# FFN1 units of four pairs and one block in 512-column steps, and a fixed order of TensorE's passes in the first third, in a fused attention and FFN kernel

## The chip, the cores and the metric

The kernel runs on one core of a Trainium2 chip. The metric is the device time of one execution in microseconds. Three runs of the kernel before took 151.54, 151.74 and 151.81 us, median 151.74. The core has a matrix engine (TensorE, PE in the profile; its weight loads are listed apart as PEld), a vector engine (DVE), a scalar engine (ACT), GpSimd (POOL), and queues that start DMAs (SP above all). Each engine works through its own list of instructions in order and waits for the others by semaphores.

## The reference

One layer norm feeds two branches, and the output is their sum with the input. S = 2048 tokens, D = 448, 16 heads of 28, F = 1792.

```
xn  = layernorm(x)                                   # no weights
q, k, v = split(xn @ wqkv)                           # per head
phi(t)  = concat(softmax(t @ w_phi), softmax(-(t @ w_phi)))
kv = phi(k)^T v ;  z = sum over tokens of phi(k)
A  = ((phi(q) kv) / (phi(q) z + 1e-6)) @ wo
B  = silu(xn @ w1) @ w2                              # FFN1, FFN2
out = x + A + B
```

All inputs and the output are bfloat16; products accumulate in float32.

## The kernel before

**Tiles.** The 2048 tokens are 16 tiles of 128, taken as 8 pairs (0 to 7). D is 3 blocks of 128 and one of 64. The normalised rows of a pair lie in `xn_sb` and are transposed on TensorE into `xnT`: `ln_pair` computes statistics (`bnst`, `bnag`, `ve` on DVE, `rstd` on GpSimd), normalises in three DVE instructions (`xn`), transposes in seven steps (`xnT_tr`) into a pair of PSUM banks, and copies these out (`xnT_ev`). PSUM has eight banks of 512 float32 columns; the code uses them in pairs.

**Steps and passes.** TensorE is used as two halves of 64 rows. A step is two matmuls that run side by side, one on each half (`mms`, line 445). `contract` (line 476) makes one product out of two passes: the first has 4 steps for each block of output, the second 3, and the second adds to what the first wrote with the halves exchanged, so all its steps wait on a semaphore until the last matmul of the first has ended (`o.syncs.add(prev.id)`). Between the two passes other work is wanted.

**FFN1.** `ffn1_chunk(p0, npair, f0, fend, units)` (line 745) makes units: one unit fills one pair of banks (2 x 512 columns) and ends in one SiLU of 1024 columns on ACT, which writes `hT`. With two pairs of tokens (`npair = 2`) a step has 256 columns and a unit holds two blocks of F; there are 14 blocks. `units` names the banks, in turn. Pairs 0 and 1 use `ffn1_single`; pairs 2 to 7 are 7 units for each two pairs, all with `npair = 2`: 13 of these 21 units come before the attention part, 8 behind its projections.

**Fold.** The weights of q and k are multiplied by w_phi on the chip: `fold_tr` transposes them in three sets of 24 matmuls (`wT_tr`), DVE copies each in two instructions (`wT_ev`) into `scr`, and `fold(kt)` multiplies (`fold_mm`, nine steps for each of four `kt`) into banks 6 and 7. Three DVE copies and one ACT copy (`fold_ev`) bring the result to `wqk_sb`.

**Attention part.** For each pair `k_macro` projects k and v (`pk_mm`, `v_mm`), `q_group` the queries (`pq_mm`, 512 columns); ACT takes exponentials (`exp_act`), DVE the sums, GpSimd the divisions, and `k_acc` adds to kv. ACT has one function table at a time: it loads the one for exponentials once, behind the last SiLU of the first part (`pre_exp`). Then the remaining FFN1 units run among the products of q and kv (`U_mm`), whose results DVE divides (`q_divide`), and last come FFN2 and the output projection pair by pair.

**Order.** A list scheduler (`schedule`, line 218) with estimated costs orders each engine's instructions; smaller numbers of an operation go first when several are ready. `odeps` fix an order within one engine without a semaphore. Before the change such fixed orders hold for the first pairs (`order0`), for the attention part (`chain`) and for the last unit with the transposes of pair 7 (`turn`, lines 920 to 923); between these (lines 879 to 919) the scheduler chooses. `ln_pair(6)` and `ln_pair(7)` stand at lines 909 and 916, behind the folds; they write banks 2 and 3, and 6 and 7. DMAs are issued in order on SP's queue, and `paced` (lines 1260 and 1261) holds some of the loads back until given copies are done.

Of the kernel before, what the change touches and what calls it, by code (L numbers as in the profile page):

```python
# [332 lines left out]
def bass_parallel_sum__linear_kernel_hedgehog__dense_activation_silu__prompt_kernel(  # L333
# [10 lines left out]
    S, D, H, DH, FF = 2048, 448, 16, 28, 1792  # L344
    NT, NPAIR = S // 128, S // 256
    KF = 3
    FT = FF // 128
# [8 lines left out]
    with es:  # L356
# [4 lines left out]
        NXN = 4  # L361
# [60 lines left out]
        P = _Prog()  # L422
# [105 lines left out]
        def warm(n, cols=256):  # L528

            one = [nc.const_aps.tensor(1.0, [64, 128], dtype=BF16, start_partition=64 * h) for h in range(2)]  # L530
            rhs = [a[:, None, :].broadcast_to([64, cols // 128, 128]) for a in one]
            dst = [banks[4 + h][:, 0:cols].rearrange("p (a c) -> p a c", c=128) for h in range(2)]
            k = len(P.ops)
            for i in range(n):
                mms([(dst[h], one[h], rhs[h], True, True) for h in range(2)], "warm", cols * 0.836)
            return P.ops[k:]
# [96 lines left out]
                    xn, x_sb[:, t, c0:c1], mv[:, t, 0:1], rstd[:, t:t + 1], ALU.subtract, ALU.mult),  # L633
                    reads=[x_sb[:, t, c0:c1], mv[:, t, 0:1], rstd[:, t:t + 1]], writes=[xn], name="xn")

        def ln_tr(p, js, b0, eng):
            for i, j in enumerate(js):
                trs([(bank16[b0 + h][:, 64 * i:64 * i + 64], xn_sb[r, p % NXN, 128 * j:128 * j + 128], r)
                     for h, r in enumerate((UP, LO))], "xnT_tr")
            n = len(js)  # L640
            src = psum16[:, b0 * 1024:(b0 + 2) * 1024].rearrange("p (b c) -> p b c", b=2)[:, :, 0:64 * n].rearrange(
                "p b (j u) -> p b j u", u=64)
            dst = xnT[:, js[0]:js[-1] + 1, p, :].rearrange("p j (b u) -> p b j u", b=2)
            if eng == "act":
                act(dst, src, ACTF.Identity, "xnT_ev")
            else:
                copy_dve(dst, src, "xnT_ev", d_dve(128 * n, 2))
# [8 lines left out]
                    reads=[xs, mv[:, tt, 0:1], rstd[:, tt:tt + 1]], writes=[dst], name="xn")  # L656

        def lnz_bank(p, t, j):
            return 6 if p else (2 * (j // 2) if t == 0 else 6 - 2 * (j // 2))

        def lnz_tr(p, t):
            k = len(P.ops)
# [61 lines left out]
                c.odeps.add(a.id)  # L724
            return ev

        def ln_pair(p, one_by_one=False):
            t0, t1 = 2 * p, 2 * p + 1
            for t in (t0, t1):
                ln_stats(t)  # L730
                if one_by_one:
                    ln_rstd(t, t + 1)
            if not one_by_one:
                ln_rstd(t0, t1 + 1)
            ln_norm(p, t0)
            ln_norm(p, t1)
            ln_tr(p, [0, 1, 2, 3, 4, 5, 6], {2: 2, 3: 4, NPAIR - 2: 2}.get(p, 6), "act" if p in LN_ACT else "dve")

        LN_ACT = (2,)
        silus = []  # L740
# [98 lines left out]
            copy_dve(wqk_sb[:, kt, 0, 0:7, 56:64], bA[:, 168:224].rearrange("p (g u) -> p g u", u=8), "fold_ev", d_dve(56))  # L839

        ev0, order0 = lnz_first()
        banks_ = iter((0, 2, 4, 0, 2, 4, 0, 6))
        evp, passes, ln_late = [], [], []
        for p in range(2):
            for f0, f1, i0, i1 in ((0, 6, 0, 2), (0, 6, 2, 3), (6, 10, 0, 2), (10, FT, 0, 2)):
# [30 lines left out]
        for a, c in zip(order0, order0[1:]):  # L876
            for o in c:
                o.odeps.add(a[-1].id)
        k = len(P.ops)
        ln_pair(4)  # L880
        later4 = [o for o in P.ops[k:] if o.eng == "dve"]
        tr4 = [o for o in P.ops[k:] if o.name == "xnT_tr"]
        evp.append(P.ops[-1])
        unit_no[0] = 0
        ffn1_chunk(2, 2, 0, 4, (4, 0, 2))
        k = len(P.ops)
        ln_pair(5)
        later5 = [o for o in P.ops[k:] if o.eng == "dve"]
        for o in later4 + later5:
            o.odeps.add(early_dve)  # L890
        for i in range(3):
            ffn1_chunk(2, 2, 4 + 2 * i, 6 + 2 * i, (4, 0, 2))
            fold_tr(3 * i)
        for o in tr4:
            o.odeps.add(units_done[2][0][-1].id)
        ffn1_chunk(2, 2, 10, FT, (4, 0, 2))
        P.cur_prio = 2
        late_constants()
        lnz_rest()
        P.cur_prio = 0  # L900
        for kt in range(4):
            ffn1_chunk(4, 2, 2 * kt, 2 + 2 * kt)
            k = len(P.ops)
            fold(kt)
            for o in P.ops[k:]:
                if o.eng == "pe":
                    o.odeps.add(units_done[-1][1][-1].id)
        k = len(P.ops)
        ln_pair(6)
        for o in P.ops[k:]:  # L910
            if o.eng == "dve":
                o.odeps.add([a for a in later4 if a.name == "xn"][-1].id)
        unit_no[0] = 0
        ffn1_chunk(4, 2, 8, 12, (0, 4))
        k = len(P.ops)
        ln_pair(7)
        for o in P.ops[k:]:
            if o.eng == "dve":
                o.odeps.add([a for a in later5 if a.name == "xn"][-1].id)
        turn = [units_done[-1][0], [o for o in P.ops if o.name == "xnT_tr"][-7:], units_done[-1][1]]  # L920
        for x, y in zip(turn, turn[1:]):
            for o in y:
                o.odeps.add(x[-1].id)

        def proj(p, W, b0, name):
            return contract([(lambda r, b: xnT[r, b, p, :], W,
# [1 line left out]

        def k_macro(p):
            sl = p % NEK  # L930
            kbk = {1: 4, 2: 6, 7: 6}.get(p, 0)
            k12 = proj(p, lambda r, k: wqk_sb[r, k, 1, :, 0:56], kbk, "pk_mm")
            kb = psum[:, kbk * 512:kbk * 512 + 1024].rearrange("p (t c) -> p t c", t=2)[:, :, 0:D]
            for s in range(2):
                exp_act(Ek[sl][:, :, s * D:(s + 1) * D], kb, 1.0 if s == 0 else -1.0, "exp_k")
            v12 = proj(p, lambda r, k: wv_sb[r, k, :], 2, "v_mm")
            vb = psum[:, 1024:2048].rearrange("p (t c) -> p t c", t=2)[:, :, 0:D].rearrange("p t (h d) -> p t h d", h=H)
# [88 lines left out]
        for p in range(NPAIR):  # L1026
# [12 lines left out]
            if p == 6:  # L1039
                chain += [k12[0], v12[0], k12[1], v12[1], k_acc(3)]  # L1040
            elif p == NPAIR - 1:
                chain += [k12[0], k_acc(4), v12[0], k12[1], v12[1], q12[0], k_acc(5), q12[1]]
            elif p > 2:
                chain += [k12[0], v12[0], k12[1], v12[1], q12[0], k_acc(p - 3), q12[1]]
            else:
# [149 lines left out]
        def marked(fn, *a):  # L1195
            k = len(P.ops)
            fn(*a)
            return [o for o in P.ops[k:] if o.eng == "pe"]

        out_order = []  # L1200

        def out_pair(p):
# [173 lines left out]
```

## Time and profile before

| what | value |
|---|---|
| runs | 151.54 to 151.81 us, median 151.74 |
| profiled execution | 151.56 us, of which the span is 149.81 us |
| first matmul of the attention part | 40.53 us from the span's start |
| FFN1, 256 columns | 744 matmuls from `xnT` and `w1_sb`, 46.0 us busy |
| weight loads of FFN1 | 768, 94 ns each |
| SiLU of a whole unit | 1.02 us each, 27 of them |

The span runs from the first to the last instruction of the core. Rows of the timeline have a start, a length, an engine, a line, the operation with output and input, their shapes, and a count of merged instructions; in brackets stands idle time ahead of the row, with what ended it. Matmuls overlap (the next starts before the last has left the array), so TensorE's pace is read from one row's start to the next row's, and a length of 0.27 us for a 256-column matmul isn't what it costs. Line 448 is the helper that issues all matmuls, so groups are told apart by tile names: `w_sb` in the profile stands for `w1_sb` and `w2_sb`, `EqT` also holds data of the first two pairs, `scr` the transposed weights.

### The profile page before, as it was taken

To read this page: it belongs to the slowest core of one execution; us is meant where nothing else is said; L and a number is where in the kernel's file an instruction comes from. 1 tells how busy PE (TensorE), PEld (TensorE's weight loads), DVE (VectorE), ACT (ScalarE), POOL (GpSimd) and SP (SyncE) were. 2 spreads that over 40 slices of the span, in tenths; PEclk is the share of its full clock that TensorE was granted. 3 is DMA by queue.
4 is the path that set the end of the run, shared out by engine and by line. 5 is a ranking of instruction groups with operands and counts; after the bars stand their busy time and mean duration, and the time that the engine had idled before them with its cause. 6 is when DMAs were issued, how large, how long until landed. Compare 5 with 4: busy or idle time off the path is not lost.

```text
span 149.8 us, 5945 instructions
## 1 busy us (share of the span) xinstructions
PE 145.9 (97%) x2698; PEld 97.1 (65%) x2698; DVE 100.1 (67%) x192; ACT 72.6 (48%) x83; POOL 56.2 (38%) x86
## 2 busy tenths in 40 slices
PE   7899999999999999999999999999999999999992
PEld 6798888888844444444488985555555555555672
DVE  1998888865518899777992677839393939392203
ACT  3657755568699887779488554202020202022000
POOL 7134131020102778876981064270707061614000
PEclk9999999999999999999999999999999999999999
DMA  4999374000004432353201000010101010101012
GB/s 120 354 263 256 100 218 131 4 4 4 4 0 123 127 123 68 87 132 45 33 4 21 4 4 0 4 61 4 61 4 61 7 61 4 61 0 66 0 66 61
DMA packets 9427, 10.30 MB, mean 69 GB/s; under 512 B 1626, under 2 KB 9018, under 8 KB 9402
## 3 DMA queue, kind: packets, MB, share of 16 engines
q1 hardware_dynamic: 9098, 9.71, 22.6%
q8 instruction: 21, 0.34, 0.9%
q10 hardware_dynamic: 304, 0.21, 0.5%
q14 instruction: 4, 0.03, 0.1%
HBM read 7.37 MB, written 1.84 MB: 61 GB/s over the span
## 4 chain that ended last, share of the span: by engine, by line
PE 94%; DVE 2%; DMA 1%; issue 0%
PE psum L448 91%; PE psum L461 3%; DMA x_sb<-in_A_x_dram 1%; DVE st L610 1%; DVE EqT L654 1%; DVE out_raw L1190 0%; DVE mv L614 0%; PE psum L1075 0%; DVE rstd L692 0%
## 5 line engine op out<-in xcount | busy, mean ns | idle before, releaser
L448 PE MATMUL psum<-xnT,w_sb 64*128 64x256 bf16 (+1 forms) x768 | 46.7, 268 | 0.0
L448 PE MATMUL psum<-w_sb,hT 64*128 64x448 bf16 (+2 forms) x504 | 46.5, 328 | 0.0
L448 PEld LDWEIGHTS psum<-xnT,w_sb 64*128 64x128 bf16 x768 | 35.5, 94 | 4.4
L467 ACT ACTIVATE hT<-psum 128x1024 bf16<-128x1024 f32 (+1 forms) x29 | 28.3, 993 | 14.4 <-PE psum L448 14.3
L1161 POOL TENSOR_TENSOR xn_sb<-wraw 128x448 bf16<-128x448 f32 (+4 forms) x39 | 20.6, 562 | 36.3 <-DVE wraw L1139 23.6
L448 PEld LDWEIGHTS psum<-w_sb,hT 64*128 64x128 bf16 x504 | 22.5, 94 | 16.6
L467 ACT ACTIVATE oT<-psum 128x896 bf16<-128x896 bf16 x8 | 7.3, 917 | 40.2 <-PE psum L461 40.2
L952 POOL TENSOR_TENSOR scr<-scr,Rk 128x1792 bf16<-128x1792 bf16 (+2 forms) x8 | 19.2, 2407 | 14.0 <-ACT scr L467 11.1
L1139 DVE TENSOR_TENSOR wraw<-psum,Gq 128x1792 f32<-128x1792 f32 (+1 forms) x10 | 16.4, 1650 | 0.9
L467 ACT ACTIVATE EqT<-psum 128x1024 bf16<-128x1024 f32 x14 | 13.6, 1021 | 3.9 <-PE psum L448 3.9
L1190 DVE TENSOR_TENSOR out_raw<-psum,x_sb 128x896 bf16<-128x896 f32 (+2 forms) x9 | 8.8, 980 | 9.5 <-PE psum L448 9.4
L1124 DVE RECIPROCAL R<-psum 128x64 f32<-128x64 f32 (+1 forms) x9 | 4.6, 511 | 15.2 <-PE psum L448 15.2
L448 PE MATMUL psum<-wv_sb,xnT 64*128 64x448 bf16 x112 | 13.7, 349 | 0.0
L448 PE MATMUL psum<-wo_sb,oT 64*128 64x448 bf16 (+2 forms) x126 | 13.6, 328 | 0.0
L448 PE MATMUL psum<-wqk_sb,xnT 64*128 64x448 bf16 x112 | 13.2, 349 | 0.0
L448 PE MATMUL psum<-xnT,wqk_sb 64*128 64x512 bf16 (+1 forms) x112 | 13.0, 378 | 0.0
L625 POOL TENSOR_TENSOR rstd<-ve,neghalf 128x2 f32<-128x2 f32 (+1 forms) x9 | 5.9, 651 | 17.4 <-DVE ve L624 17.4
L944 DVE TENSOR_REDUCE Sk<-scr 128x64 f32<-128x1792 bf16 (+1 forms) x8 | 12.3, 1532 | 0.2
L610 DVE BATCH_NORM_STATS2 st<-x_sb 128x6 f32<-128x448 bf16 x16 | 9.8, 615 | 3.2 <-DMA x_sb<-in_A_x_dram 3.2
L467 ACT ACTIVATE scr<-psum 128x896 bf16<-128x896 f32 x12 | 10.3, 913 | 2.4 <-PE psum L448 1.8
L471 DVE CAST scr<-psum 128x896 bf16<-128x896 f32 x6 | 6.5, 1080 | 6.2 <-PE psum L448 6.2
L448 PEld LDWEIGHTS psum<-wo_sb,oT 64*128 64x128 bf16 x126 | 5.9, 94 | 4.8 <-ACT oT L467 0.2
(78 smaller groups left out, 133.7 us busy)
## 6 DMA issues: line engine op xcount, KB each, us to landing
out_dram<-out_raw SPq DMA_DIRECT2D x7, 224.0 KB, 1.9
w_sb<-in_B_w_dram SPq DMA_DIRECT2D x3, 448.0 KB, 3.4
x_sb<-in_A_x_dram SPq DMA_DIRECT2D x2, 448.0 KB, 5.3
w_sb<-in_B_w_dram SPq DMA_DIRECT2D x2, 384.0 KB, 5.7
x_sb<-in_A_x_dram SPq DMA_DIRECT2D x3, 224.0 KB, 5.1
w_sb<-in_B_w_dram SPq DMA_DIRECT2D x3, 224.0 KB, 3.9
wraw<-in_A_wqkv_dram SPq DMA_DIRECT2D x1, 672.0 KB, 4.4
w_sb<-in_B_w_dram SPq DMA_DIRECT2D x1, 576.0 KB, 4.2
```

Of the source, the lines that this page charges most:

```text
L448: r = e.matmul(dst, lhsT, rhs, start=start, stop=stop, skip_group_check=True)
L461: out = e.transpose(dst, src, ident[r, 64:128] if r == LO else ident[r, 0:64])
L467: return P.op("act", d_act(_cols(src)), lambda e: e.activation(dst, src, func, scale=scale), reads=[src], writes=[dst], table=table, name= ...
L471: return P.op("dve", dur, lambda e: e.tensor_copy(dst, src), reads=[src], writes=[dst], name=name)
L610: P.op("dve", 600, lambda e: e.bn_stats(st6[:, t, :], x_sb[:, t, :]), reads=[x_sb[:, t, :]], writes=[st6[:, t, :]], name="bnst")
L625: P.op("pool", 580, lambda e: e.tensor_tensor(r2, v2, nh, ALU.pow), reads=[v2, nh], writes=[r2], name="rstd")
L944: P.op("dve", d_dve(896 * n), lambda e, S4=S4, E4=E4: e.tensor_reduce(S4, E4, AXL.X, ALU.add), reads=[E4], writes=[S3], name="Sk")
L952: lambda e, E5=E5, R5=R5: e.tensor_tensor(E5, E5, R5, ALU.mult),
L1124: P.op("dve", d_rec(32 * n), lambda e, R3=R3, U=U: e.reciprocal(R3, U[:, :, :, DH + 1]), reads=[U[:, :, :, DH + 1]], writes=[r2], name="R2")
L1139: P.op("dve", d_dve(896 * m), lambda e, dsto=dsto, Uj=Uj, Gj=Gj, m=m: e.tensor_tensor(dsto, Uj[:, :, :, 0:DH], Gj[:, :, :, None].broadcast ...
L1161: lambda e, dst=dst, a0=a0, a1=a1: e.tensor_tensor(dst, a0, a1, ALU.add),
L1190: P.op("dve", d_dve(2 * (c1 - c0)), lambda e: e.tensor_tensor(dst, ob, xs, ALU.add), reads=[ob, xs], writes=[dst], name="out_ev")
```

## The change

Of the 21 units of pairs 2 to 7, twelve get four pairs and one block (`npair = 4`): a step then has 512 columns and a unit 7 steps in place of 14. They are blocks 10 to 13 of pairs 2 to 5, and blocks 2 to 9 of pairs 4 to 7 (2 to 4 before the attention part, 5 to 9 behind it). Blocks 0 to 9 of pairs 2 and 3, blocks 0 and 1 of pairs 4 and 5, and blocks 0, 1 and 10 to 13 of pairs 6 and 7 stay in 256 columns. The counts on both sides of the attention part are as before, 13 units and 8.

Since units of pairs 4 to 7 now come before the attention part, pairs 6 and 7 are normalised and transposed ahead of the folds. Their transposes share one pair of banks (0 and 1, at column offsets 0 and 448); `ln_ev` is split off from `ln_tr` and copies both behind pair 7's transposes. A list `mid` fixes the order of all of TensorE's passes from the first unit of pairs 2 and 3 to the attention part; a list `turn` fixes DVE's order of weight copies, statistics, normalisation and the two pairs' copies; the last SiLU is put behind the last `fold_ev` on ACT. The banks of the first units are renamed, and in the attention part the banks of k, v and some queries are exchanged and pair 0 projects v ahead of k. No wait is added but those that follow from the data and the banks.

```diff
-            dst = [banks[4 + h][:, 0:cols].rearrange("p (a c) -> p a c", c=128) for h in range(2)]
+            dst = [banks[2 + h][:, 0:cols].rearrange("p (a c) -> p a c", c=128) for h in range(2)]
...
-        def ln_tr(p, js, b0, eng):
+        def ln_tr(p, js, b0, c0=0):
...
+        def ln_ev(p, j0, j1, b0, eng, c0=0):
...
-            return 6 if p else (2 * (j // 2) if t == 0 else 6 - 2 * (j // 2))
+            return 6 if p else ((4, 0) if t == 0 else (6, 2))[j // 2]
...
-            ln_tr(p, [0, 1, 2, 3, 4, 5, 6], {2: 2, 3: 4, NPAIR - 2: 2}.get(p, 6), "act" if p in LN_ACT else "dve")
+            b0 = {2: 0, 3: 2, 6: 0, 7: 0}.get(p, 6)
+            ln_tr(p, [0, 1, 2, 3, 4, 5, 6], b0, 448 if p == 7 else 0)
+            if ev:
+                ln_ev(p, 0, 7, b0, "act" if p in LN_ACT else "dve")
...
-        banks_ = iter((0, 2, 4, 0, 2, 4, 0, 6))
+        banks_ = iter((4, 0, 2, 4, 0, 2, 4, 6))
...
+        tr4, later4 = ln_later(4, early_dve)
+        evp.append(later4[-1])
+        k = len(units_done)
         unit_no[0] = 0
-        ffn1_chunk(2, 2, 0, 4, (4, 0, 2))
...
+        ffn1_chunk(2, 2, 0, 4, (2, 4, 0))
+        tr5, later5 = ln_later(5, early_dve)
+        ftr = []
         for i in range(3):
-            ffn1_chunk(2, 2, 4 + 2 * i, 6 + 2 * i, (4, 0, 2))
-            fold_tr(3 * i)
...
-        ffn1_chunk(2, 2, 10, FT, (4, 0, 2))
+            ffn1_chunk(2, 2, 4 + 2 * i, 6 + 2 * i, (2, 4, 0))
+            ftr.append(marked(fold_tr, 3 * i))
+        unit_no[0] = 0
+        ffn1_chunk(2, 4, 10, FT, (0, 2, 4, 2))
+        ffn1_chunk(4, 2, 0, 2, (4,))
+        tr6, later6 = ln_later(6, last_xn(later4), False)
+        tr7, later7 = ln_later(7, last_xn(later5), False)
+        k2 = len(P.ops)
+        ln_ev(6, 0, 7, 0, "dve", 0)
+        ln_ev(7, 0, 7, 0, "dve", 448)
+        ev67 = P.ops[k2:]
...
         for kt in range(4):
-            ffn1_chunk(4, 2, 2 * kt, 2 + 2 * kt)
...
+            if kt:
+                ffn1_chunk(4, 4, 1 + kt, 2 + kt, (0, 2, 4))
+            folds.append(marked(fold, kt))
+        A, Q, B, C = units_done[k:k + 5], units_done[k + 5:k + 9], units_done[k + 9], units_done[k + 10:]
+        mid = [A[0][0], A[1][0], A[0][1], A[2][0], A[1][1], A[3][0], tr4, A[2][1], A[4][0], tr5, A[3][1], A[4][1], ftr[0], Q[0][0], Q[1][0], Q[0][1], ftr[1], Q[1][1], Q[2][0], tr6, Q[2][1], tr7, Q[3][0], ftr[2],
+               Q[3][1], B[0], folds[0], B[1], C[0][0], folds[1], C[1][0], C[0][1], folds[2], C[2][0], C[1][1], folds[3], C[2][1]]
+        for a, c in zip(mid, mid[1:]):
+            for o in c:
+                o.odeps.add(a[-1].id)
+        silus[-1].odeps.add([o for o in P.ops if o.name == "fold_ev" and o.eng == "act"][-1].id)
+        wev = [o for o in P.ops if o.name == "wT_ev"]
+        x6, x7 = ([o for o in ops if o.name == "xn"] for ops in (later6, later7))
+        stats = [o for o in later7 if o.name in ("bnst", "bnag", "ve")]
+        turn = wev[0:2] + stats[1:] + x6 + x7 + wev[2:4] + ev67 + wev[4:]
+        for a, c in zip(turn, turn[1:]):
+            c.odeps.add(a.id)
...
-            kbk = {1: 4, 2: 6, 7: 6}.get(p, 0)
+            kbk = {1: 4, 2: 6, 7: 6}.get(p, 2)
...
-            v12 = proj(p, lambda r, k: wv_sb[r, k, :], 2, "v_mm")
+            v12 = proj(p, lambda r, k: wv_sb[r, k, :], 0, "v_mm")
...
-            qb = {1: 0, 2: 4, 6: 0}.get(4 * ch + c, 6)
+            qb = {1: 2, 2: 4, 6: 2}.get(4 * ch + c, 6)
...
-                chain += [k12[0], v12[0], k12[1], v12[1][:1], q12[0], v12[1][1:], q12[1]]
+                chain += [v12[0], k12[0], v12[1][:2], k12[1], q12[0], v12[1][2:], q12[1]]
...
-        ffn1_chunk(4, 2, 12, FT, (6,))
+        ffn1_chunk(6, 2, 0, 2, (6,))
+        ffn1_chunk(6, 2, 10, FT, (2, 0))
         unit_no[0] = 0
-        ffn1_chunk(6, 2, 0, FT, (2, 0, 6, 0, 6, 0, 6))
+        ffn1_chunk(4, 4, 5, 10, (6, 0))
```

`ln_later` is `ln_pair` with its DVE instructions put behind a given one; `marked` returns the TensorE operations that a function issues; `last_xn` gives the last normalising instruction of a pair.

More of the change, by code (lines that the diff above doesn't have):

```diff
@@ L634, in ln_norm @@
                     reads=[x_sb[:, t, c0:c1], mv[:, t, 0:1], rstd[:, t:t + 1]], writes=[xn], name="xn")
-        def ln_tr(p, js, b0, eng):
+        def ln_tr(p, js, b0, c0=0):
             for i, j in enumerate(js):
-                trs([(bank16[b0 + h][:, 64 * i:64 * i + 64], xn_sb[r, p % NXN, 128 * j:128 * j + 128], r)
+                trs([(bank16[b0 + h][:, c0 + 64 * i:c0 + 64 * i + 64], xn_sb[r, p % NXN, 128 * j:128 * j + 128], r)
                      for h, r in enumerate((UP, LO))], "xnT_tr")
-            n = len(js)
-            src = psum16[:, b0 * 1024:(b0 + 2) * 1024].rearrange("p (b c) -> p b c", b=2)[:, :, 0:64 * n].rearrange(
+        def ln_ev(p, j0, j1, b0, eng, c0=0):
+            n = j1 - j0
+            src = psum16[:, b0 * 1024:(b0 + 2) * 1024].rearrange("p (b c) -> p b c", b=2)[:, :, c0:c0 + 64 * n].rearrange(
                 "p b (j u) -> p b j u", u=64)
-            dst = xnT[:, js[0]:js[-1] + 1, p, :].rearrange("p j (b u) -> p b j u", b=2)
+            dst = xnT[:, j0:j1, p, :].rearrange("p j (b u) -> p b j u", b=2)
             if eng == "act":
@@ L725, in lnz_second, with ln_pair @@
             return ev
-        def ln_pair(p, one_by_one=False):
+        def ln_pair(p, one_by_one=False, ev=True):
             t0, t1 = 2 * p, 2 * p + 1
@@ L878, in bass_parallel_sum__linear_kernel_hedgehog__dense_activation_silu__prompt_kernel, with ln_later, last_xn, marked @@
                 o.odeps.add(a[-1].id)
[L879 to L883, printed above, removed]
-        unit_no[0] = 0
-        ffn1_chunk(2, 2, 0, 4, (4, 0, 2))
[L886 to L890, printed above, removed]
-        for i in range(3):
-            ffn1_chunk(2, 2, 4 + 2 * i, 6 + 2 * i, (4, 0, 2))
-            fold_tr(3 * i)
-        for o in tr4:
-            o.odeps.add(units_done[2][0][-1].id)
-        ffn1_chunk(2, 2, 10, FT, (4, 0, 2))
+        def ln_later(p, behind, ev=True):
+            k = len(P.ops)
+            ln_pair(p, ev=ev)
+            ops = P.ops[k:]
+            for o in ops:
+                if o.eng == "dve":
+                    o.odeps.add(behind)
+            return [o for o in ops if o.name == "xnT_tr"], [o for o in ops if o.eng == "dve"]
+        def last_xn(ops):
+            return [o for o in ops if o.name == "xn"][-1].id
+        def marked(fn, *a):
+            k = len(P.ops)
+            fn(*a)
+            return [o for o in P.ops[k:] if o.eng == "pe"]
+        tr4, later4 = ln_later(4, early_dve)
+        evp.append(later4[-1])
+        k = len(units_done)
+        unit_no[0] = 0
+        ffn1_chunk(2, 2, 0, 4, (2, 4, 0))
+        tr5, later5 = ln_later(5, early_dve)
+        ftr = []
+        for i in range(3):
+            ffn1_chunk(2, 2, 4 + 2 * i, 6 + 2 * i, (2, 4, 0))
[9 more added lines that the diff above has]
+        ev67 = P.ops[k2:]
         P.cur_prio = 2
@@ L900, in bass_parallel_sum__linear_kernel_hedgehog__dense_activation_silu__prompt_kernel @@
         P.cur_prio = 0
+        unit_no[0] = 0
+        folds = []
         for kt in range(4):
-            ffn1_chunk(4, 2, 2 * kt, 2 + 2 * kt)
[L903 to L923, printed above, removed]
+            if kt:
[14 more added lines that the diff above has]
+            c.odeps.add(a.id)
         def proj(p, W, b0, name):
@@ L935, in k_macro @@
                 exp_act(Ek[sl][:, :, s * D:(s + 1) * D], kb, 1.0 if s == 0 else -1.0, "exp_k")
-            v12 = proj(p, lambda r, k: wv_sb[r, k, :], 2, "v_mm")
-            vb = psum[:, 1024:2048].rearrange("p (t c) -> p t c", t=2)[:, :, 0:D].rearrange("p t (h d) -> p t h d", h=H)
+            v12 = proj(p, lambda r, k: wv_sb[r, k, :], 0, "v_mm")
+            vb = psum[:, 0:1024].rearrange("p (t c) -> p t c", t=2)[:, :, 0:D].rearrange("p t (h d) -> p t h d", h=H)
             copy_dve(vaug[sl][:, :, :, 0:DH], vb, "v_ev", d_dve(896))
@@ L1044, in bass_parallel_sum__linear_kernel_hedgehog__dense_activation_silu__prompt_kernel @@
                 chain += [k12[0], v12[0], k12[1], v12[1], q12[0], k_acc(p - 3), q12[1]]
+            elif p:
+                chain += [k12[0], v12[0], k12[1], v12[1][:1], q12[0], v12[1][1:], q12[1]]
             else:
-                chain += [k12[0], v12[0], k12[1], v12[1][:1], q12[0], v12[1][1:], q12[1]]
+                chain += [v12[0], k12[0], v12[1][:2], k12[1], q12[0], v12[1][2:], q12[1]]
         sums = [o for o in P.ops if o.name in ("Sk", "Rk")][-8:]
@@ L1193, in out_store @@
                   name="out_dma", out_slot=slot)
[L1195 to L1198, printed above, removed]
         out_order = []
```

## The prediction

> **What bounds the kernel now.** I read the page first: busy shares, granted clock, shares of the chain that ended last.
>
> ```profile
> span 149.8 us, 5945 instructions
> PE 145.9 (97%) x2698; PEld 97.1 (65%) x2698; DVE 100.1 (67%) x192; ACT 72.6 (48%) x83; POOL 56.2 (38%) x86
> PEclk9999999999999999999999999999999999999999
> PE 94%; DVE 2%; DMA 1%; issue 0%
> ```
>
> TensorE is busy for 97% of the span, at full granted clock in every slice, and 94% of the last chain is its own work. So the change is worth what it takes out of the PE row or adds to it; the other engines matter where PE waits for them. Then the timeline: PE's rows of the stretch that is rewritten (start, length, engine, instruction, count). Spacing is read from start to start, since the lengths contain the pipeline's tail.
>
> ```profile
> 25.30 0.55 PE L461 MATMUL psum<-ident,wraw 64*128 64x64 bf16 x24
> ...
> 27.45 0.51 PE L461 MATMUL psum<-ident,wraw 64*128 64x64 bf16 x24
> 27.80 1.83 PE L448 MATMUL psum<-xnT,w_sb 64*128 64x256 bf16 x30
> ...
> 31.80 0.34 PE L448 MATMUL psum<-BD,scr 64*128 64x56 bf16 x14
> 31.98 0.27 PE L448 MATMUL psum<-xnT,w_sb 64*128 64x256 bf16 x1
> ...
> 32.03 1.93 PE L448 MATMUL psum<-xnT,w_sb 64*128 64x256 bf16 x31
> 33.80 0.34 PE L448 MATMUL psum<-BD,scr 64*128 64x56 bf16 x14
> ...
> 37.28 1.03 PE L448 MATMUL psum<-xnT,w_sb 64*128 64x256 bf16 x15
> 38.22 0.38 PE L461 MATMUL psum<-ident,xn_sb 64*128 64x64 bf16 x14
> 38.43 1.36 PE L448 MATMUL psum<-xnT,w_sb 64*128 64x256 bf16 x22
> 39.63 0.37 PE L461 MATMUL psum<-ident,xn_sb 64*128 64x64 bf16 x14
> 39.86 0.83 PE L448 MATMUL psum<-xnT,w_sb 64*128 64x256 bf16 x12
> 40.53 0.92 PE L448 MATMUL psum<-wqk_sb,xnT 64*128 64x448 bf16 x8
> ```
>
> The attention part begins at 40.53. From 25.30 to there 15.23 us pass. They hold 230 narrow (256-column) FFN1 matmuls (the first row of them is the 32 that follow 25.30, the last the 12 at 39.86), three sets of weight transposes, four folds and the transposes of pairs 6 and 7.
>
> **Prices.** Clean streams of both widths:
>
> ```profile
> 83.31 1.70 PE L448 MATMUL psum<-xnT,w_sb 64*128 64x256 bf16 x28
> 84.84 0.39 PE L448 MATMUL psum<-KVZ,EqT 56*128 56x60 bf16 x16
> ```
> ```profile
> 46.96 1.03 PE L448 MATMUL psum<-xnT,wqk_sb 64*128 64x512 bf16 x8
> 47.82 0.54 PE L448 MATMUL psum<-wv_sb,xnT 64*128 64x448 bf16 x4
> 48.20 0.81 PE L448 MATMUL psum<-xnT,wqk_sb 64*128 64x512 bf16 x6
> 48.85 0.92 PE L448 MATMUL psum<-wqk_sb,xnT 64*128 64x448 bf16 x8
> ```
>
> A narrow matmul takes 1.53/28 = 0.0546 us, a wide one (0.86+0.65)/14 = 0.1079 (the query's; FFN1 has no wide one yet). Two narrow for one wide save 1.3 ns. Weight transposes take 27.80-27.45 = 0.35, a pair's transposes 38.43-38.22 = 0.21, a fold 0.18 (31.80 to 31.98, when 14 of its 16 have gone) to 0.23 (to 32.03).
>
> Before, without waits: 230 x 0.0546 = 12.56, plus 1.05, 0.42 and 0.72 to 0.92, together 14.75 to 14.95. The trace has 15.23, so 0.28 to 0.48 us are waits. One of them has its name:
>
> ```profile
> 38.22 0.26 PEld L461 LDWEIGHTS psum<-ident,xn_sb 64*128 64x128 bf16 x14 [0.18 <-ACT hT L467]
> ```
>
> Pair 6's transposes write banks 2 and 3 and wait there for a SiLU. The others lie in the runs after folds: 31 narrow from 32.03 to 33.80 take 1.77 instead of 1.69. There the planner puts a unit's second pass, which waits until its first has ended, two steps behind it.
>
> On the Trainium skill, "TensorE: Matmul & The Clock Gate", section "Back-to-back issue gap": it gives about 81 ns per matmul at 128 columns and 131 at 512 for streams that load weights for each, by which (an estimate) some 64 ns per matmul don't depend on the width, and 168 fewer matmuls would save 5 us or more. The narrow row above contradicts this (54.6 ns with two running side by side), so the sum doesn't use it.
>
> **The change, part by part.**
>
> *Wide steps before 40.53.* 98 wide matmuls replace 196 narrow ones: 10.70-10.57 = 0.13 us saved.
>
> *Set order.* In the changed program's instruction order the same stretch holds 34 narrow (1.86), 98 wide (10.57), and the same transposes and folds: 14.62 to 14.82 us without waits, against 15.23. No second pass stands within two steps of its first, and the transposes of pairs 6 and 7 write bank 0, whose SiLU is done earlier. New: pair 6's transposes alone part the third wide unit's passes. What that costs, from the groups by shape (count, busy us, mean ns):
>
> ```profile
> L448 PE MATMUL psum<-xnT,w_sb 64*128 64x256 bf16 x744 | 46.0, 269 | 0.0
> ...
> L448 PE MATMUL psum<-xnT,wqk_sb 64*128 64x512 bf16 x84 | 11.1, 377 | 0.0
> ```
>
> Before, pair 7's transposes part the passes of the last unit in the same way: its last narrow step starts at 39.63-0.11 = 39.52, its second pass at 39.86, 0.34 later, which is the length 0.269 and 0.07. A wide step needs 0.377+0.07 = 0.45 and PE is there after 0.216+0.21 = 0.43: I take 0.03 of wait, which cancels against the one before (0.23 from 39.63, where 38.22 to 38.43 took 0.21).
>
> *Who must be in time.* Rows for DVE, GpSimd and ACT:
>
> ```profile
> 26.00 1.02 DVE L471 COPY scr<-psum 128x768 bf16<-128x768 bf16 x2 [0.35 <-PE psum L461]
> 29.19 0.59 DVE L610 BATCH_NORM_STATS2 st<-x_sb 128x6 f32<-128x448 bf16 x1
> 31.31 0.17 DVE L624 TENSOR_SCALAR ve<-mv 128x2 f32<-128x2 f32 x1
> 31.56 0.69 POOL L625 TENSOR_TENSOR rstd<-ve,neghalf 128x2 f32<-128x2 f32 x1 [1.03 <-DVE ve L624]
> 33.16 0.88 DVE L632 TENSOR_SCALAR xn_sb<-x_sb,mv,rstd 128x448 bf16<-128x448 bf16 x3
> 40.14 0.62 DVE L471 COPY xnT<-psum 128x896 bf16<-128x896 bf16 x1 [0.79 <-PE psum L461]
> ```
>
> On the old clock PE reaches: first weight transposes 25.63 (six narrow moved ahead of them), second 28.35, pair 6's transposes 30.21, pair 7's 31.1, third weight transposes 32.17, first fold 34.04. DVE follows 0.70 behind the transposes (26.00-25.30): first copies 26.33 to 27.35, what is left of pair 7's statistics to 28.45 (0.59, 0.17, and two aggregates taken as long as that), pair 6 normalised by 29.35, pair 7 by 30.25 (its rstd at 28.3+0.25+0.69 = 29.2), both 0.85 early. Second copies to 31.3 (needed at 32.17), then pair 7's transposes are awaited (39.63 to 40.14 behind their start) and both pairs copied by 31.1+0.51+1.24 = 32.85, third copies 32.87 to 33.9. The first fold needs those 0.15 to 0.3 later: DVE's tightest place. Price if this cover goes: what DVE is late, PE is late.
>
> ```profile
> 38.06 0.49 ACT L467 ACTIVATE wqk_sb<-psum 128x392 bf16<-128x392 f32 x1
> 40.73 1.02 ACT L467 ACTIVATE hT<-psum 128x1024 bf16<-128x1024 f32 x1 [0.41 <-PE psum L448]
> 41.78 1.28 ACT L467 ACT_TABLE_LOAD   x1
> 43.18 1.71 ACT L467 ACTIVATE scr<-psum 128x896 bf16<-128x896 f32 x2
> ```
>
> The last SiLU is now put behind the last fold's copy, itself behind the SiLU before; behind it wait the table load and all exponentials. With X the start of the attention part, the last SiLU began at X+0.20 and the exponentials at X+2.65. Now the unit before ends a fold and six wide matmuls ahead of X (0.23+0.65 = 0.88); its SiLU begins 0.20 behind that, at X-0.68, and ends at X+0.34, the copy at X+0.83, the last SiLU at X+1.85, the load at X+3.13; with 0.12 from load to exponential, as before, X+3.25, 0.6 later. The first bank wanted back is the query's of pair 1 (46.96 = X+6.43), released 1.71 behind that, at X+4.96, so it costs nothing. The fourth fold meets the third one's ACT copy within 0.05; I take 0.03.
>
> *Moved at no price.* Banks of the first units are only renamed. Pair 4's copy comes 16 narrow matmuls later (0.87) and paces the value weights' DMAs and, behind them on SP's queue, the tail copy; it lies ahead of 25.30, and their user stands at X. Putting v ahead of k for pair 0 leaves one v step instead of two between the query's passes: 0.216+0.19 = 0.41 us where 0.45 is needed, 0.04 lost.
>
> *Late stretch.* 70 wide for 140 narrow, 0.09 saved on paper, but three of the five units lie between products that DVE paces:
>
> ```profile
> 87.40 1.09 DVE L1139 TENSOR_TENSOR wraw<-psum,Gq 128x896 f32<-128x896 f32 x1
> ...
> 88.54 0.28 PEld L448 LDWEIGHTS psum<-KVZ,EqT 56*128 56x128 bf16 x16 [0.27 <-DVE wraw L1139]
> ```
>
> DVE ends at 88.49 and the product starts at 88.54; a faster PE waits longer there. 0.02 is left.
>
> **Sum.** Width 0.13; waits removed 0.28 to 0.48, of which I take 0.35, nearer the low end because a fold costs PE most of 0.23 wherever it stands; fold 0.03 and query 0.04 given back; late 0.02. 0.13+0.35-0.07+0.02 = 0.43, rounded down to 0.40 for small waits in the new order. The profiled execution took 151.56 (1.76 around its span), the runs 151.74 (median), 0.18 more. 151.56-0.40 = 151.16 there, 151.3 as a median. Bounds: all waits gone and the late 0.09 kept is 0.70, or 151.05; the low end with 0.25 of new waits is 0.16, or 151.6.
>
> **Rivals.**
> *New pass waits.* Six places now have wide steps with one block of 0.2 between a unit's passes (pair 6's transposes, those of kv, three products, the query). At 0.04 each 0.25 goes: 151.55. For it: 39.63 to 39.86. Against: block and tail grow together.
> *DVE becomes the bound at the first fold.* 12 more DVE steps stand before it. If they run 0.5 late, the fold waits 0.25 to 0.35: 151.6; at 1 us late, 152.1. Against: its rows there show 0.35 and 0.79 of idle time.
> *Slower: wide steps at a higher price.* In one row they have it:
>
> ```profile
> 60.49 1.03 PE L448 MATMUL psum<-xnT,wqk_sb 64*128 64x512 bf16 x8
> 61.45 0.39 PE L448 MATMUL psum<-scr 128*32 128x56 bf16 x32
> ```
>
> 0.96/8 = 0.1196, 0.0117 above my price, on 168 matmuls 1.97 us: 153.3. It decides from 0.1103 on (0.40/168 more); at 0.1121 the kernel is 0.2% slower. Against: a change of array shape follows this row, and the two clean rows agree.
> *More than forecast*: 0.6 to 0.7, 151.1.
> *By the skill's rule* 5 us: about 146.5.
> That the change isn't what it says is excluded: the instruction order has the 168 wide matmuls.
>
> **Chances.** Forecast 0.64, more 0.08, pass waits 0.12, DVE 0.07, dear wide steps 0.08, the rule 0.01. 0.2% (0.30 us, 151.44) is about what a measurement of this kernel tells from no change. Faster: 0.60 of the forecast, 0.08 and 0.01, 0.69. Same: 0.04 of the forecast, 0.12, 0.04 of DVE, 0.20. Slower: 0.03 and 0.08, 0.11. The range 151.0 to 151.8 leaves out the dear steps, the slower part of DVE and the rule, with a little below. The likeliest case's own is 151.1 to 151.5.
>
> **What would show it.** The v matmuls of pair 0 start near 40.1; wide FFN1 rows at 0.108 per matmul; no idle time of the weight loads before pair 6's and 7's transposes; the first fold not later than 34.1; the exponentials up to 3.25 behind X; the third product's wait for DVE 0.05 longer. Wrong if wide matmuls cost over 0.110, if PE waits for DVE before a fold, or if X moves by less than 0.2.

## The result, and the profile after

The changed kernel takes 151.25 us (median of 22 runs, 150.94 to 151.91) where the kernel before, on the same chip, takes 151.77 (22 runs, 151.37 to 152.47): a ratio of 0.997, 95% interval 0.9958 to 0.9981. The prediction was 151.3. The profiled execution took 151.52 us, of which the span is 149.7.

The page of the changed kernel, first part, clock and chain:

```profile
span 149.7 us, 5611 instructions
PE 146.1 (98%) x2530; PEld 91.6 (61%) x2530; DVE 100.2 (67%) x192; ACT 72.5 (48%) x83; POOL 56.4 (38%) x86
PEclk9999999999999999999999999999999999999999
PE 94%; DVE 3%; issue 0%; DVEq 0%
```

TensorE still sets the end. It has 168 matmuls fewer and is shown as busy as before (146.1 against 145.9 us): busy time is a union of overlapping lengths, and a wait shorter than a matmul's length can hide in it, so it doesn't show the gain. Starts of rows do. The groups by shape:

```profile
L448 PE MATMUL psum<-xnT,w_sb 64*128 64x256 bf16 x408 | 25.0, 269 | 0.0
L448 PE MATMUL psum<-xnT,w_sb 64*128 64x512 bf16 x168 | 20.8, 376 | 0.0
```

The timeline of TensorE in the changed kernel, from the first unit of pairs 2 and 3 to the second pass of pair 0's queries:

```profile
17.79 4.97 PE L448 MATMUL psum<-xnT,w_sb 64*128 64x256 bf16 x88
22.59 0.37 PE L461 MATMUL psum<-ident,xn_sb 64*128 64x64 bf16 x14
...
25.84 0.51 PE L461 MATMUL psum<-ident,wraw 64*128 64x64 bf16 x24
26.19 2.54 PE L448 MATMUL psum<-xnT,w_sb 64*128 64x512 bf16 x22
28.56 0.51 PE L461 MATMUL psum<-ident,wraw 64*128 64x64 bf16 x24
28.91 1.68 PE L448 MATMUL psum<-xnT,w_sb 64*128 64x512 bf16 x14
30.43 0.37 PE L461 MATMUL psum<-ident,xn_sb 64*128 64x64 bf16 x14
30.65 0.82 PE L448 MATMUL psum<-xnT,w_sb 64*128 64x512 bf16 x6
31.31 0.37 PE L461 MATMUL psum<-ident,xn_sb 64*128 64x64 bf16 x14
31.51 1.03 PE L448 MATMUL psum<-xnT,w_sb 64*128 64x512 bf16 x8
...
34.25 0.40 PE L448 MATMUL psum<-BD,scr 64*128 64x56 bf16 x16
...
40.30 1.00 PE L448 MATMUL psum<-wv_sb,xnT 64*128 64x448 bf16 x8
...
42.76 1.10 PE L448 MATMUL psum<-xnT,wqk_sb 64*128 64x512 bf16 x8
43.62 0.43 PE L448 MATMUL psum<-wv_sb,xnT 64*128 64x448 bf16 x2
43.93 0.82 PE L448 MATMUL psum<-xnT,wqk_sb 64*128 64x512 bf16 x6
```

And the row of the kernel before that stands where the first of these does:

```profile
17.47 4.14 PE L448 MATMUL psum<-xnT,w_sb 64*128 64x256 bf16 x72
```

A wide FFN1 matmul takes (28.56-26.19)/22 = 0.108 us, the price of the query's. No weight-load row of pair 6's or pair 7's transposes has idle time ahead of it now. In the kernel before, 15 narrow matmuls took 0.94 from 37.28 to pair 6's transposes at 38.22, 0.12 over their price; here 14 wide ones take 1.52 from 28.91 to those transposes at 30.43, and their price is 1.51. The attention starts at 40.30 against 40.53, but this execution reached the rewritten stretch 0.32 us later. Three places serve as marks for every kernel here: S, the first matmul of the units of pairs 2 and 3; X, the first of the attention; F, the first of FFN2 (all from the timeline, us).

| kernel | S | X | F | X-S | F-S |
|---|---|---|---|---|---|
| before | 17.47 | 40.53 | 89.44 | 23.06 | 71.97 |
| changed | 17.79 | 40.30 | 89.32 | 22.51 | 71.53 |
| changed, twice more | 18.11, 17.95 | 40.62, 40.46 | 89.63, 89.48 | 22.51, 22.51 | 71.52, 71.53 |
| wide steps as halves | 17.49 | 40.12 | 89.15 | 22.63 | 71.66 |
| second pass directly behind | 18.23 | 40.98 | 90.00 | 22.75 | 71.77 |
| query passes parted | 17.70 | 40.21 | 89.17 | 22.51 | 71.47 |
| last SiLU not held back | 17.55 | 40.06 | 89.56 | 22.51 | 72.01 |
| order alone, old units | 17.90 | 41.18 | 90.10 | 23.28 | 72.20 |
| planner's order, new units | 17.69 | - | 91.00 | - | 73.31 |
| two places altered (two runs) | 17.45, 17.76 | 39.93, 40.23 | 88.89, 89.20 | 22.48, 22.47 | 71.44, 71.44 |

So the change gains 0.55 us by X and has 0.44 left at F; from F on (FFN2) both kernels have the same work. The distances repeat within 0.01 us from one execution to the next, where whole times scatter by 1 us; the lowest times of both kernels (151.37 and 150.94) differ by 0.43, much as the distances do.

### The profile page after: what moved, and what is told of

Same layout as the page of the kernel before. It is cut to its first block, busy times and chain, and to the rows that moved or that the text cites. A ratio compares the mean times of both kernels' runs of the same rounds, so it can differ in the third digit from the quotient of the medians.

```text
span 149.7 us, 5611 instructions
## 1 busy us (share of the span) xinstructions
PE 146.1 (98%) x2530; PEld 91.6 (61%) x2530; DVE 100.2 (67%) x192; ACT 72.5 (48%) x83; POOL 56.4 (38%) x86
## 4 chain that ended last, share of the span: by engine, by line
PE 94%; DVE 3%; issue 0%; DVEq 0%
PE psum L448 91%; PE psum L461 3%; DVE wraw L1160 1%; DVE R L1145 0%; DVE rden L1152 0%; DVE out_raw L1211 0%; DVE Gq L1153 0%; DVE Dd L1147 0%; DVE den L1149 0%; PE psum L1096 0%; DVEq L1333 0%
## 5 line engine op out<-in xcount | busy, mean ns | idle before, releaser
L448 PE MATMUL psum<-xnT,w_sb 64*128 64x256 bf16 (+2 forms) x600 | 46.3, 297 | 0.0
L448 PEld LDWEIGHTS psum<-xnT,w_sb 64*128 64x128 bf16 x600 | 27.9, 94 | 8.6
```

The source lines that it names most:

```text
L448: r = e.matmul(dst, lhsT, rhs, start=start, stop=stop, skip_group_check=True)
```

## The experiments

**The changed kernel again**, beside the next three.

> The changed kernel again, as it is, so that the other runs have it beside them. Theory: time about 0.9966 of the kernel before; from the first matmul of pairs 2 and 3 to the first matmul of the attention 22.51 us as in the profile of after (23.06 before), and the 0.3 us by which that stretch began later in the profile of after (17.79 against 17.47) was that execution's own: it begins near 17.5 here or is seen to differ from execution to execution. Rival: the banks moved at the start cost 0.3 us, and the stretch begins at 17.8 again.

Measured: ratio 0.9975 (0.9959 to 0.9992), X-S 22.51. S lay at 18.11 here, and in the ten traces of the same opening code anywhere from 17.45 to 18.23 (the table), so the 0.32 of the profile of after was that execution's: the rival falls. The old opening code scatters as well: 17.47 in the profile of before, 17.90 in the run with the old units. One thing that moves S is seen on DVE, in the run with S at 18.11:

```profile
13.07 0.63 DVE L610 BATCH_NORM_STATS2 st<-x_sb 128x6 f32<-128x448 bf16 x1 [0.67 <-DMA x_sb<-in_A_x_dram]
```

In the profile of before the same instruction starts at 12.43, behind 0.24 us of idle time. It waits for a load of x; it starts 0.64 later here, and S lies 0.64 later too.

**Wide steps as halves.** Every step of 512 columns becomes two of 256; units, banks, order and SiLUs stay.

```diff
-                for ft in range(f0, f1):
+                for i in range(f0 * n, f1 * n, 256):
+                    ft, q0, c = i // n, p0 + i % n // 128, i - f0 * n
...
-                                 [banks[b0 + par][:, (ft - f0) * n:(ft - f0) * n + n] for par in range(2)],
-                                 ft == f0, True))
+                                 [banks[b0 + par][:, c:c + 256] for par in range(2)],
+                                 c == 0, True))
-                units_done.append(contract(jobs, n, True, True, "ffn1_mm"))
+                units_done.append(contract(jobs, 256, True, True, "ffn1_mm"))
```

> The changed kernel with every step of 512 columns issued as two of 256: same units, banks, order and SiLUs. Theory (order and waits carry most of the gain): the stretch from the first matmul of pairs 2 and 3 to the attention grows by 98 wide matmuls x (2 x 0.0546 - 0.1079 = 0.0013) = 0.13 us, 22.51 to 22.64; the late five units grow by up to 0.09, of which the wait for VectorE ahead of the last product takes most; time 0.9975 of the kernel before, 0.1 to 0.2 us over the changed kernel. Rival (the width is the whole gain): stretch back at 23.0 to 23.1, time 1.000 of the kernel before.

Measured: X-S 22.63, 0.12 more, as the first theory had it to 0.01; ratio 0.999 (0.9975 to 1.0004), with the 0.9975 expected at its edge. F-X is 49.03 against 49.02: the late 70 wide steps are worth 0.01. The reason is in the rows of this kernel ahead of the last product:

```profile
87.11 1.09 DVE L1161 TENSOR_TENSOR wraw<-psum,Gq 128x896 f32<-128x896 f32 x1
...
88.25 0.28 PEld L448 LDWEIGHTS psum<-KVZ,EqT 56*128 56x128 bf16 x16 [0.27 <-DVE wraw L1161]
```

and in those of the changed kernel:

```profile
87.28 1.09 DVE L1160 TENSOR_TENSOR wraw<-psum,Gq 128x896 f32<-128x896 f32 x1
...
88.43 0.28 PEld L448 LDWEIGHTS psum<-KVZ,EqT 56*128 56x128 bf16 x16 [0.55 <-DVE wraw L1160]
```

In both the product starts 0.05 to 0.06 behind DVE's end (88.20 and 88.37); the wide steps only lengthen the idle time ahead of it. So of the 0.55 at X, 0.12 is the width and 0.43 is what this kernel still has over the one before: order, banks, earlier normalisation. No run splits the 0.43 among these three.

**A second pass directly behind its first**, in the first unit of four pairs (part of the list `mid`):

```diff
-Q[0][0], Q[1][0], Q[0][1], ftr[1],
+Q[0][0], Q[0][1], Q[1][0], ftr[1],
```

> The changed kernel with one second pass put directly behind its first: the first unit with four pairs, whose second pass stood behind the next unit's first pass. Theory (a second pass may start no sooner than the start of the last matmul of its first pass plus that matmul's own length, 0.38 us at 512 columns, plus 0.07): a wait of 0.38 + 0.07 - 0.22 = 0.23 us there, the attention 0.23 later, time 0.2 us (0.0015) over the changed kernel. Rival (the 0.06 to 0.07 us waits of before were all that such a place costs, whatever the distance): 0.07 us.

Measured: X-S 22.75, F-S 71.77, 0.24 more in both; ratio 1.000 (0.9983 to 1.0018). The place itself, in this kernel:

```profile
26.63 2.78 PE L448 MATMUL psum<-xnT,w_sb 64*128 64x512 bf16 x22
...
27.72 1.19 PEld L448 LDWEIGHTS psum<-xnT,w_sb 64*128 64x128 bf16 x14 [0.56 <-PE psum L448]
```

The 22 matmuls take 2.62 us (the next row starts at 29.25) where they took 2.37. The theory's 0.23 holds, and the rival's 0.07 falls: here, too, the second pass started about one matmul's length and 0.07 us behind the start of the last matmul of its first (0.216+0.24 = 0.46, against 0.377+0.07 = 0.45), as it did at 256 columns in the kernel before (0.34, against 0.269+0.07).

**Query passes parted.** Two steps of pair 1's k stand between the passes of pair 0's query group in place of one step of v.

```diff
-                chain += [k12[0], v12[0], k12[1], v12[1][:1], q12[0], v12[1][1:], q12[1]]
+                chain += ([k12[0][:2], q0, k12[0][2:]] if p == 1 else [k12[0]]) + [v12[0], k12[1], v12[1][:1], q12[0], v12[1][1:], q12[1]]
...
-                chain += [v12[0], k12[0], v12[1][:2], k12[1], q12[0], v12[1][2:], q12[1]]
+                q0 = q12[1]
+                chain += [v12[0], k12[0], v12[1], k12[1], q12[0]]
```

> The changed kernel, only the order of pair 0's projections differs: between the two passes of its first query group stand two steps of pair 1's K instead of one step of pair 0's V. Theory (the second pass was issued too close behind its first, 0.12 us in the profile of after): the wait goes, and no other second pass waits in its place; the attention's first 4.3 us shorten by 0.12, time 0.1 us (0.0007) under the changed kernel. Rival (the wait moves to the next second pass, K of pair 0 or of pair 1, or a transfer or exponential paces there): the same time as the changed kernel within 0.03.

Measured: the wait goes, and pair 1's query starts 6.43 behind X (46.64) where it was 6.56 (46.86). At F only 0.06 is left (71.47): two later places give half of it back, so theory and rival hold in part. The time, ratio 0.9987 (0.9971 to 1.0003) beside 0.9975 for the changed kernel, can't tell 0.06. Rows of this kernel:

```profile
42.85 1.11 PE L448 MATMUL psum<-xnT,wqk_sb 64*128 64x512 bf16 x8
...
44.10 0.89 PE L448 MATMUL psum<-xnT,wqk_sb 64*128 64x512 bf16 x6
...
48.52 1.00 PE L448 MATMUL psum<-wqk_sb,xnT 64*128 64x448 bf16 x8
49.30 0.54 PEld L448 LDWEIGHTS psum<-wv_sb,xnT 64*128 64x128 bf16 x8 [0.22 <-DVE scr L471]
49.31 0.97 PE L448 MATMUL psum<-wv_sb,xnT 64*128 64x448 bf16 x8
...
54.80 0.77 PE L448 MATMUL psum<-wv_sb,xnT 64*128 64x448 bf16 x6
55.51 1.06 PE L448 MATMUL psum<-xnT,wqk_sb 64*64 64x512 bf16 x16
```

The k group takes 49.31-48.52 = 0.79 where it took 0.76 (48.75 to 49.51): v then waits for DVE to clear its bank (the row of weight loads at 49.30). The v steps ahead of the change of array shape take 0.71, where they took 0.66 (54.99 to 55.65). The lengths tell why the latter: rows of eight and six wide matmuls last 1.11 and 0.89 here, where clean ones last 1.03 and 0.81. One half of the array runs some 0.08 us behind the other (the rows that show this stand with the query's term below), and what waits for both halves pays for the later one.

**The last SiLU not held back** on ScalarE behind the last fold copy:

```diff
-        silus[-1].odeps.add([o for o in P.ops if o.name == "fold_ev" and o.eng == "act"][-1].id)
```

> The changed kernel without the one line that puts the last SiLU of the stretch behind the last fold copy on ScalarE; the order on TensorE is the same. Theory (that line is the cover: K of pair 0 needs the fourth fold's copy 0.76 us after the attention starts): the SiLU goes first, the copy ends about 0.9 us later, and K of pair 0 waits 0.4 to 0.6 us; time 0.3 to 0.5 us (0.002 to 0.003) over the changed kernel. Rival (ScalarE has room there, as the prediction had it for the exponentials): the same time, and the exponentials 0.5 us sooner behind the attention's start.

Measured: X-S 22.51 as before, F-S 72.01, 0.48 more; ratio 0.9995 (0.9974 to 1.0015): the change without this one line gains nothing that can be told. Rows of this kernel:

```profile
39.46 1.94 ACT L467 ACTIVATE hT<-psum 128x1024 bf16<-128x1024 f32 x2 [0.33 <-PE psum L448]
...
40.82 0.81 PE L448 MATMUL psum<-wqk_sb,xnT 64*128 64x448 bf16 x6
41.28 0.50 ACT L467 ACTIVATE wqk_sb<-psum 128x392 bf16<-128x392 f32 x1
...
41.93 0.37 PE L448 MATMUL psum<-wqk_sb,xnT 64*128 64x448 bf16 x2 [0.30 <-ACT wqk_sb L467]
```
```profile
43.06 1.04 PE L448 MATMUL psum<-xnT,wqk_sb 64*128 64x512 bf16 x8
43.93 0.37 PE L448 MATMUL psum<-wv_sb,xnT 64*128 64x448 bf16 x2
44.17 0.82 PE L448 MATMUL psum<-xnT,wqk_sb 64*128 64x512 bf16 x6
```

Two SiLUs run ahead of the copy, and k of pair 0 waits for it: its eight matmuls take 42.12-40.82 = 1.30 where they took 0.76 (0.54 lost). After that long wait the halves start nearly level again (the wide row lasts 1.04), and the same query places that cost 0.12 in the changed kernel cost 0.05: the v pair takes 0.24 (43.93 to 44.17) in place of 0.31.

**Order alone, in the kernel before.** Its own units, banks and normalisation; around the folds the order is set so that second passes stand four steps behind their first. `V` holds the units of pairs 4 and 5, `f` the folds, `tr6` and `tr7` the transposes of pairs 6 and 7; the list replaces the old `turn`, and the lines that set up these names aren't shown.

```diff
+        turn = [V[0][0], V[2][0][2:6], V[0][1], f[0], V[1][0], V[2][0][6:] + V[3][0][:2], V[1][1], f[1], V[3][0][2:6], V[2][1], f[2],
+                V[3][0][6:], V[5][0][:4], V[3][1], f[3], V[4][0], V[5][0][4:6], tr6, V[4][1], V[5][0][6:], tr7, V[5][1]]
```

> The kernel before with its own units of 256 columns, banks and normalisation, and only the order of TensorE around the folds set so that each second pass of pairs 4 and 5 stands four steps behind its first instead of two. Theory (the order needs the new units and banks: steps taken early use up the time that ScalarE's SiLUs and copies had): the three waits of 0.06 to 0.07 us at second passes go, but waits for ScalarE come in their place at the folds and at K of pair 0; the stretch from 17.47 to 40.53 (23.06 us) does not shorten, it grows by 0.1 to 0.5. Rival (order alone brings it, without new units): the stretch shortens by 0.19 to 0.35.

Measured: X-S 23.28, 0.22 more than the kernel before; ratio 1.001 (0.9993 to 1.0027). Rows of this kernel:

```profile
36.11 0.09 PEld L448 LDWEIGHTS psum<-BD,scr 64*128 64x128 bf16 x1 [0.28 <-DVE wqk_sb L471]
...
41.18 0.49 PEld L448 LDWEIGHTS psum<-wqk_sb,xnT 64*128 64x128 bf16 x8 [0.28 <-ACT hT L467]
```

Steps taken early to part one unit's passes are missing later: the third fold comes before DVE has cleared its banks, and k before ScalarE has cleared its own. Another order of the old units might do better; this one doesn't.

**The planner's order, in the changed kernel** (the list scheduler chooses): the list `mid` is not applied.

```diff
-        for a, c in zip(mid, mid[1:]):
-            for o in c:
-                o.odeps.add(a[-1].id)
```

> The changed kernel with its new units, banks and order on VectorE, but without the written order on TensorE for that stretch: the planner chooses it. Theory (the order is what keeps second passes, folds and transposes from waiting): second passes wait again and work waits for VectorE's and ScalarE's copies, the attention 0.3 us later or more, time no better than the kernel before (0.999 or more). Rival (width and banks bring the gain, any order does): within 0.1 us of the changed kernel.

Measured: ratio 1.0072 (1.0046 to 1.0098), F-S 1.78 more than in the changed kernel. Rows of this kernel:

```profile
35.95 0.33 PEld L448 LDWEIGHTS psum<-xnT,w_sb 64*128 64x128 bf16 x6 [0.73 <-DVE xnT L471]
...
43.37 0.10 PEld L448 LDWEIGHTS psum<-wqk_sb,xnT 64*128 64x128 bf16 x2 [0.91 <-DVE wqk_sb L471]
```

A wide unit of pairs 4 to 7 comes before DVE has copied the transposes of pairs 6 and 7, and later k of pair 0 waits for a copy of a fold. The banks and DVE's order were laid out for the list, so this is what the list is worth in this kernel, not what an order is worth in general.

**Two places altered**: the query passes as above, and pair 7's transposes beside pair 6's (part of the list `mid`).

```diff
-tr6, Q[2][1], tr7, Q[3][0], ftr[2],
+tr6, tr7, Q[2][1], Q[3][0], ftr[2],
```

> The changed kernel with two places of its order altered: two steps of pair 1's K between the passes of the first query group, as in the run before, and the transposes of pair 7 beside those of pair 6, both between the passes of one unit. Theory: the 0.03 us wait of that unit's second pass goes (the stretch to the attention 22.51 to 22.48), the query's 0.12 goes, of which 0.06 is given back by the sixth pair of the attention; time 0.09 us (0.0006) under the changed kernel, ratio to the kernel before about 0.9966 where the changed kernel stands at 0.9972. Rival: pair 7 is normalised too late for its transposes, and they wait as long as the place saves.

Measured: X-S 22.48, F-S 71.44, 0.09 under the changed kernel; ratio 0.9951 (0.9933 to 0.9969). Then once more, with the changed kernel on the same chip:

> The changed kernel once more, beside the altered version on the same chip. Theory: ratio to the kernel before 0.997 to 0.9975, as in the two comparisons so far, and from the first matmul of pairs 2 and 3 to the first FFN2 matmul 71.52 us.

> The version with the two altered places (pair 7's transposes beside pair 6's, two steps of pair 1's K between the passes of the first query group) once more, beside the changed kernel on the same chip. Theory: 71.44 us over the same stretch as in its first trace, 0.08 to 0.09 under the changed kernel, and so 0.05 to 0.1 us less time; rival: a difference of times that small is lost in the scatter of the runs (over 0.2 us either way).

Measured: 151.28 us, ratio 0.9946 (0.9927 to 0.9965), for the altered version, and 151.48, 0.9965 (0.9946 to 0.9984), for the changed kernel. The intervals overlap, so the times don't part the two; the distances do, 71.44 in both traces against 71.52 to 71.53 in three. This version is under the kernel before by its times, and under the changed one by 0.09 us by the distance alone. The place of the transposes in it, on TensorE:

```profile
30.09 0.57 PE L461 MATMUL psum<-ident,xn_sb 64*128 64x64 bf16 x28
30.50 1.68 PE L448 MATMUL psum<-xnT,w_sb 64*128 64x512 bf16 x14
```

28 transposes take 0.41; in the changed kernel the two sets took 0.22 and 0.20, and pair 7's are normalised in time: the rival falls.

## Why the prediction was right, and which of its terms were not

The sum of 0.40 came out at 0.44 by the distances, and its mechanism held: waits are the larger part, the width the smaller. Term by term:

- *Width before the attention*, 0.13 forecast: 0.12, shown by the halves. The price of a wide step was right (0.108), so the rival of dear wide steps falls, and with it the rule of the Trainium skill, "TensorE: Matmul & The Clock Gate", section "Back-to-back issue gap", as far as it was used here: 98 matmuls fewer in this stretch saved 0.12 us, not microseconds.
- *Waits removed*, 0.35 less 0.03 for a fold. From 25.30 to X the prediction's own stretch took 15.23; now, with the six narrow matmuls put ahead of it (0.33), it is 40.30-(25.84-0.33) = 14.79, so 0.44 less, 0.12 of it width: 0.32, as forecast. That this is waits, and not dearer or cheaper work, goes by the prices, which held (0.0546, 0.108); one such wait is seen in rows, the 0.12 ahead of pair 6's transposes. What failed is the boundary. The set order begins at S, and the sum began at 25.30. Between the two the kernel before takes 25.30-17.47 = 7.83, the changed one 25.51-17.79 = 7.72: 0.11 that the prediction left out. The rows show part of it: 72 narrow took 3.97 (0.0551 each), 0.04 over their price, where now 88 take 4.80 (0.0546).
- *The query of pair 0*, 0.04 forecast: 0.12. The v pair takes 0.31 where two matmuls take 0.19. The spacing rule was right (0.45 needed, 0.41 there); it took both halves to run level. Behind the folds they don't: the query's eight matmuls last 1.10, not 1.03. Rows of the changed kernel at the last fold, and the query's wait:

```profile
39.44 0.37 PE L448 MATMUL psum<-BD,scr 64*128 64x56 bf16 x13
39.65 0.37 PE L448 MATMUL psum<-xnT,w_sb 64*128 64x512 bf16 x1
39.66 0.23 PE L448 MATMUL psum<-BD,scr 64*128 64x56 bf16 x3
39.73 0.81 PE L448 MATMUL psum<-xnT,w_sb 64*128 64x512 bf16 x5
...
43.93 0.33 PEld L448 LDWEIGHTS psum<-xnT,wqk_sb 64*128 64x128 bf16 x6 [0.34 <-PE psum L448]
```

One half starts its wide matmul at 39.65, the other only at 39.73, behind three more matmuls of the fold. With these 0.08 the later half is the one that counts: 0.04+0.08 = 0.12. Parting the passes took the wait away, and in the run without ScalarE's order, where the halves were nearly level, it was 0.05, close to the forecast.

- *Late stretch*, 0.02 forecast: 0.01. The last product waits for DVE, as the prediction said, and takes what the width saves.
- *Own second pass behind pair 6's transposes*, 0.03 forecast: 0.22 (30.43 to 30.65) against 0.20 for pair 7's.
- *The new pass waits at six places*, a rival: 0.02 at pair 6's transposes, 0.12 at the query, and nothing to be seen at the others together: from pair 1's first query to F the changed kernel takes 42.46 (46.86 to 89.32), the kernel before 42.48 (46.96 to 89.44).
- *DVE at the first fold*, the tightest place by the prediction. Rows of DVE in the changed kernel:

```profile
28.51 1.86 DVE L632 TENSOR_SCALAR xn_sb<-x_sb,mv,rstd 128x448 bf16<-128x448 bf16 x6
30.29 1.01 DVE L471 COPY scr<-psum 128x768 bf16<-128x768 bf16 x2
...
33.10 1.02 DVE L471 COPY scr<-psum 128x768 bf16<-128x768 bf16 x2
```

Both pairs are normalised by 30.37, ahead of pair 6's transposes at 30.43 and pair 7's at 31.31; the third copies end at 34.12 and the fold starts at 34.25. The slack of 0.13 lies just under the 0.15 to 0.3 forecast; the cover held.

- *ScalarE.* The exponentials were to start at X+3.25 at most and to cost nothing:

```profile
40.62 0.49 ACT L467 ACTIVATE wqk_sb<-psum 128x392 bf16<-128x392 f32 x1
40.99 1.03 ACT L467 ACTIVATE hT<-psum 128x1024 bf16<-128x1024 f32 x1
...
43.45 1.71 ACT L467 ACTIVATE scr<-psum 128x896 bf16<-128x896 f32 x2
```

They start at X+3.15, and nothing waits. The prediction asked what this order costs, and not what would happen without it: 0.48 us, as much as the whole change gains.

So 0.12 + 0.32 + 0.11 at X, less 0.12 at the query, plus 0.01 late, makes 0.44. The omitted 0.11 and the query's extra 0.08 nearly cancel; the nearness of 0.40 to 0.44 owes something to that, and so is partly luck.

## What to carry to other kernels

Price a fixed order by its waits, over the whole stretch that it fixes, from its first instruction on, and ask of every line of order what would stand there without it. In these traces a second pass on the same accumulator started one matmul's length and some 0.07 us behind the start of the last matmul of its first, counted on the half of the array that runs later; less that last step's own time (0.216 at 512 columns, 0.11 at 256), about 0.23 us of other work has to stand between the two. Where runs scatter more than a change is worth, distances between marks in the trace tell what the times can't.

## What the runs showed of the hardware

- The two halves of TensorE don't stay level: a row of eight wide matmuls lasted 1.10 to 1.11 us behind the folds, 1.03 to 1.04 after a wait that both halves shared. The lag costs nothing until something waits for both. The rows show it at the last fold (39.65 and 39.73 above), and the upper half has nine of a fold's sixteen matmuls, the lower seven; that an even fold would leave no lag wasn't tried.
- A wait can be worth what it costs later: removing the query's 0.12 us left 0.06 at F, since the level start that it gave was gone too (pair 1's query lasted 1.10 us in place of 1.03).
- In the traced executions of the changed kernel, scatter of the whole comes from the opening: spans of 149.7, 149.9 and 150.0 us go with S at 17.79, 17.95 and 18.11, and F-S repeats within 0.01. The same opening code reached S between 17.45 and 18.23 us in ten traces. In the two with the latest S, 18.11 and 18.23, DVE idles for a load of x (0.67 and 0.79 us); the cause in the others is open.
